# Pairs of the first MLP: three buffers for split weight forms, outputs written over copies, and conversion steps spread by time

## The chip, the core and the metric

The kernel runs on one core of a Trainium2 chip. The metric is the device time of one execution in microseconds (us). The profile is that of one further execution, taken by the hardware profiler.

## What is computed

An attention over a small state is followed by two MLPs. The 4608 rows (8 blocks of 512 sequence rows and 32 state rows) have 512 columns, and each MLP goes to 2048 columns and back.

```python
scores = scale * np.matmul(x, state.transpose(0, 1, 3, 2))
...
xread = np.matmul(a, state)
...
sread = np.matmul(a2, x)
x = np.concatenate([xread, sread], axis=2).transpose(0, 2, 1, 3).reshape(B * S, H * D)
h = x @ moe_w_in;  x = np.maximum(h, 0.0) ** 2 @ moe_w_out
h = x @ moe2_w_in; g = np.where(h > 0.0, h, np.exp(np.minimum(h, 0.0)) - 1.0)
return g @ moe2_w_out
```

All is float32 in its result, and the weights arrive as 64-bit numbers.

## The kernel before

**Precision.** A float32 operand is split into a rounded high part and a low remainder: ScalarE copies (L176), VectorE subtracts (L177). A product of two such operands is three matmuls (`product`, L41; L171 to L173).

**Stages.** Blocks 0 and 1 run alone. Blocks 2 to 7 run as three pairs of blocks (`pair`, L652), and this is the stage that the change touches. The 256 state rows follow, then the second MLP for all blocks.

**A pair.** 32 hidden steps (`h_step`, L657) make the hidden values: TensorE multiplies, ScalarE applies relu and square (L665, L666). Then the output product is made from seven products of 2 x 2 blocks instead of eight (`out_products`, L49): forms 1, 2, 6, 5, 7, 4, 3, each of eight steps. A step loads one weight (`weight1`, L645, tile `wr`, eight buffers), splits one operand into `gp` (four buffers) and runs six matmuls. Forms 6, 7 and 3 need a difference of hidden values first (`sub`, L82 and L83, on VectorE). Sums that are needed again are copied out of PSUM (L73, pools `eu` and `u2`) and later added into an output tile `o` (`added`, L76, L79; pool `oo1`, two buffers), which is stored (L678). The 16 last hidden steps run beside the first 16 product steps. The last 16 product steps of the first and second pair run beside the first eight hidden steps of the next pair, two to each.

**Conversion in the background.** The second MLP's weights are converted meanwhile, in 14 pairs of slices (`conv_pair`, L284). The raw slice (`raw`, two buffers) is read by L229 and L231 on ScalarE and becomes a float32 slice `cv` in four VectorE instructions; two more raw slices are asked for (`next_load`), the slices are stored as `d`, four sums are made (`sums`, L262), and `put_split` (L272) splits seven forms in four pieces. Each piece is copied by ScalarE into a tile `wf` (L279), subtracted by VectorE (L280) and stored (L281). In this stage `wf` has one buffer: `depth.update(raw=2, wf=1, cv=2)`. The code between two `yield` is run by one call of `next_conv` (L330). A pair takes seven calls.

**The order of the work.** Python lists `bg[i]` say what is called at step i: i below 16 is a hidden step, 16 to 31 a hidden step with a product step, 32 to 71 a product step alone. `CALLS = [27, 33, 40]` calls are spread evenly over the 72 steps of each pair (L699, L700). A scheduler then orders each engine's instructions by its own estimate of times. Every engine, and SyncE's queue of DMA issues (SP), runs its instructions in that order: one that waits holds up those behind it.

Of the kernel before, what the change touches and what calls it, by code (L numbers as in the profile page):

```python
# [34 lines left out]
HI, LO = 0, 1  # L35
SINGLE = 2
IN_SINGLE = 2
CALLS = [27, 33, 40]


def product(nc, ps, w, x, last, start):  # L41
# [7 lines left out]
def out_products(nc, split, g, weight, unit, put, sbuf, psum):  # L49


    gp_p, eu_p, u2_p, oo_p = sbuf
    tt, act = nc.vector.tensor_tensor, nc.scalar.activation
    count = iter(range(NF * HF))

    def phase(f, src, ps, start, combine=None):
        for j in range(HF):
            jj, r = divmod(j, 2)
            if combine and r == 0:
                combine(jj)  # L60
            if r % unit == 0:
                t = gp_p.tile([P, 2, unit, S], F32R, name="gp", tag="gp")
                split(t[:, HI], t[:, LO], src[jj][:, r:r + unit])
            w = weight(j, f)
            for m in range(2):
                sl = slice(m * P, (m + 1) * P)
                product(nc, ps[m], [(w[:, HI, sl], w[:, LO, sl])], [(t[:, HI, r % unit], t[:, LO, r % unit])],
                        j == HF - 1, start and j == 0)
            yield next(count)

    def copied(ps, p, name):
        t = p.tile([P, S], F32, name=name, tag=name)
        act(out=t, in_=ps, func=AF.Copy)  # L73
        return t

    def added(e, half, ps, u):  # L76
        for m in range(2):
            o = oo_p.tile([P, S], F32, name="o", tag="o")
            tt(out=o, in0=ps[m], in1=u[m], op=ALU.add)  # L79
            put(e, 2 * half + m, o)  # L80

    def sub(out, a, b):  # L82
        return lambda jj: tt(out=out[jj], in0=a[jj], in1=b[jj], op=ALU.subtract)  # L83

    a11, a12, a21, a22 = (g[q] for q in (11, 12, 21, 22))
    def banks(n):
        return [psum[n].tile([P, S], F32, name="xyz"[n], tag="xyz"[n]) for _ in range(2)]

    x = banks(0)
    yield from phase(1, a11, x, True)  # L90
    p1 = [copied(t, eu_p, "eu") for t in x]
    y = banks(1)
    yield from phase(2, a12, y, True)
    added(0, 0, y, p1)
    yield from phase(6, a11, x, False, sub(a11, a21, a11))
    u2 = [copied(t, u2_p, "u2") for t in x]
    z = banks(2)
    yield from phase(5, a21, z, True)
    yield from phase(7, a21, x, False, sub(a21, a22, a11))
    u3 = [copied(t, eu_p, "eu") for t in x]  # L100
    added(1, 1, z, u3)
    yield from phase(4, a22, x, False)
    for m in range(2):
        o = oo_p.tile([P, S], F32, name="o", tag="o")
        act(out=o, in_=x[m], func=AF.Copy)
        put(1, m, o)
    yield from phase(3, a12, z, False, sub(a12, a12, a11))
    added(0, 1, z, u2)


@with_exitstack
def attn_mlp_kernel(ctx: ExitStack, tc: tile.TileContext, xt, xn, st, w1, v1, w2, v2, outx, outs):
# [69 lines left out]
    if True:  # L182
# [88 lines left out]

        def put_split(w, srcs):  # L272

            first = 0
            for n, src in srcs:
                yield
                h = turn("wf", [P, n, 2, 256], F32R, "wf")
                with tc.issue_after(pace[0].ins):
                    nc.scalar.activation(out=h[:, :, HI], in_=src, func=AF.Copy)  # L279
                nc.vector.tensor_tensor(out=h[:, :, LO], in0=src, in1=h[:, :, HI].bitcast(F32), op=ALU.subtract)  # L280
                nc.sync.dma_start(out=w[:, first:first + n], in_=h.bitcast(F32))  # L281
                first += n

        def conv_pair(name, j):  # L284

# [1 line left out]
            v = [conv_p["cv"].tile([P, 512], F32, name="cv", tag="cv") for _ in range(2)]  # L287
            for _ in zip_longest(convert(name, j, v[0]), convert(name, j + HF, v[1])):
                yield
            next_load()  # L290
            next_load()
            d = wd[name, j] = dram.tile([P, 2, 512], F32, name=f"d_{name}{j}", tag=f"d_{name}{j}")
            for r in range(2):
                nc.sync.dma_start(out=d[:, r], in_=v[r])
            for t in sums(v):
                yield
            w = wf[name, j] = dram.tile([P, NF, 2, 256], F32, name=f"f_{name}{j}", tag=f"f_{name}{j}")
            yield from put_split(w, ((1, v[0][:, :256].unsqueeze(1)), (2, v[1].rearrange("p (q f) -> p q f", q=2)),
                                     (2, t[:, :2]), (2, t[:, 2:])))
# [266 lines left out]
        for b in range(SINGLE):  # L566
# [16 lines left out]
            else:  # L583
# [1 line left out]
                at(5, emit_m, b, 2)  # L585
                at(9, emit_m, b, 3)
                for i in range(18):
                    for _ in range(int('211212112112112110'[i])):
                        at(i, next_conv)
            at(13, emit_m, nb, 0)  # L590
            if nb < SINGLE:
# [42 lines left out]
        gq1_p = [pool(f"gq{q}", FC // 4) for q in range(4)]  # L634
        gap(pool, "gap4", 48)
        gp1_p = pool("gp1", 4)
        wr1_p = pool("wr1", 8)
        turns.update(raw=0, wf=0)
        depth.update(raw=2, wf=1, cv=2)
        conv_p.update(raw=pool("raw2", 1), cv=pool("cv2", 2), tf=pool("tf2", 1))  # L640
        eu1_p = pool("eu1", 2)
        u21_p = pool("u21", 2)
        oo1_p = pool("oo1", 2)
        ps_y, ps_x, ps_z = [pool(n, 2, space=bass.MemoryType.PSUM) for n in ("psy1", "psx1", "psz1")]
        def weight1(j, f):  # L645
            t = wr1_p.tile([P, 2, 256], F32R, name="wr", tag="wr")
# [5 lines left out]
        def pair(b0, bg, order):  # L652
# [25 lines left out]
                nc.sync.dma_start(out=x2d[b0 + e][:, k], in_=o)  # L678

            def products():  # L680
                for n in out_products(nc, split, g, weight1, 1, put, (gp1_p, eu1_p, u21_p, oo1_p), (ps_x, ps_y, ps_z)):
                    background(FC + n)
                    yield n

# [8 lines left out]
        for p, b in enumerate(pairs):  # L693
# [2 lines left out]
            def at(i, fn, *a):  # L696
                bg[i].append(lambda: fn(*a))

            for i in range(72):  # L699
                for _ in range((i + 1) * CALLS[p] // 72 - i * CALLS[p] // 72):  # L700
                    at(i, next_conv)
            for q in range(1, 4):
                at(4 * q - 3, emit_m, b, q)
                at(4 * q + 13, emit_m, b + 1, q)
# [387 lines left out]
```

## Time and profile before

| what | value |
|---|---|
| runs | 1345.14 us median of 3 (1344.6 to 1348.93) |
| the profiled execution | 1353.65 us, span 1351.9 us |
| TensorE (PE) | busy 1311.6 us, 97% |
| VectorE (DVE) | busy 968.0 us, 72% |
| ScalarE (ACT) | busy 877.4 us, 65% |
| DMA | 320.09 MB, mean 237 GB/s |

The span reaches from the first to the last instruction. Matmuls are pipelined and their ends are modelled, so a busy TensorE isn't always at its peak; its idle time and its granted clock tell more. Releasers of a wait are inferred from semaphores.

### The profile page before, as it was taken

The numbers are of one execution on the slowest core, as the hardware profiler recorded it, in microseconds if no ns is written. First come the engines' busy times: TensorE is split into PE (matmuls) and PEld (weight loads), VectorE is DVE, ScalarE is ACT, GpSimd is POOL, SyncE is SP. The second block draws the span as 40 slices with busy tenths as digits, with TensorE's granted clock in tenths as the row PEclk, the third lists the DMA queues.
The fourth block names the chain that finished last, engine by engine and source line by source line (L and its number), as shares of the span: only waits on it lengthen the run. The fifth ranks groups of instructions, "written<-read, shape, count | busy, mean of one in ns | idle before, by whom it ended". The sixth has DMA issues, their size and how long they took to land.

```text
span 1351.9 us, 19819 instructions
## 1 busy us (share of the span) xinstructions
PE 1311.6 (97%) x6972; PEld 1041.1 (77%) x6972; DVE 968.0 (72%) x1441; ACT 877.4 (65%) x1489; POOL 0.7 (0%) x6
## 2 busy tenths in 40 slices
PE   8999999999998999978999999999999999999999
PEld 6677766767666676767898888888888888888889
DVE  6988875897578975786656884569637894468645
ACT  5996768766775678754556843567446854576444
POOL 0000000000000000000000000000000000000000
PEclk9999999999999999989999999999999999999999
DMA  7999794588666886688977677876787777778733
GB/s 261 319 317 385 279 316 159 149 307 285 216 199 201 293 257 204 199 282 252 325 244 244 193 210 220 272 194 191 214 263 227 198 218 222 210 194 286 223 121 119
DMA packets 150002, 320.09 MB, mean 237 GB/s; under 512 B 15632, under 2 KB 36112, under 8 KB 146832
## 3 DMA queue, kind: packets, MB, share of 16 engines
q1 hardware_dynamic: 149904, 318.83, 74.3%
q8 instruction: 56, 0.92, 0.3%
q14 instruction: 42, 0.34, 0.1%
HBM read 242.22 MB, written 76.55 MB: 236 GB/s over the span
## 4 chain that ended last, share of the span: by engine, by line
PE 72%; DMA 9%; DVE 7%; ACT 5%; issue 1%; SPq 1%; ACTq 0%; DVEq 0%
PE x L45 20%; PE X L45 13%; PE z L45 9%; PE Z L45 6%; PE y L45 4%; PE Y L45 3%; PE h L171 3%; PE h L173 3%; PE h L172 2%; DMA f_w<-wf 2%; DMA raw_v<-in_v_dram 2%; PE as L45 2%; PE mp L350 1%; PE hs L45 1%; PE acc L171 1%
## 5 line engine op out<-in xcount | busy, mean ns | idle before, releaser
L45 PE MATMUL x<-gp,wr 128*128 128x512 f32 x1344 | 329.1, 398 | 15.2 <-DVE gp L177 9.6
L177 DVE TENSOR_TENSOR gp<-g,gp 128x512 fp32r<-128x512 f32 (+1 forms) x280 | 250.3, 901 | 124.3 <-ACT gp L176 123.0
L176 ACT ACTIVATE gp<-g 128x512 fp32r<-128x512 f32 (+1 forms) x280 | 221.3, 800 | 151.9 <-PE x L45 83.7
L45 PEld LDWEIGHTS x<-gp,wr 128*128 128x128 f32 x1344 | 254.2, 191 | 80.2 <-DVE gp L177 13.7
L45 PE MATMUL X<-xf,wr 128*128 128x512 f32 x768 | 186.6, 390 | 0.0
L45 PEld LDWEIGHTS X<-xf,wr 128*128 128x128 f32 x768 | 143.5, 188 | 31.5 <-ACT u L878 1.1
L45 PE MATMUL z<-gp,wr 128*128 128x512 f32 x672 | 157.6, 391 | 2.0 <-DMA wr<-p_v 1.5
L45 PEld LDWEIGHTS z<-gp,wr 128*128 128x128 f32 x672 | 126.2, 189 | 32.3 <-DVE gp L177 2.7
L874 DVE SCALAR_TENSOR_TENSOR g<-r,g 128x512 f32<-128x512 f32 x96 | 63.9, 689 | 65.1 <-ACT r L873 65.1
L171 PE MATMUL h<-at,m 128*128 128x512 f32 x256 | 103.4, 405 | 6.1 <-ACT m L176 3.9
L83 DVE TENSOR_TENSOR g<-g,g 128x1024 f32<-128x1024 f32 x84 | 102.1, 1219 | 0.6
L173 PE MATMUL h<-at,m 128*128 128x512 f32 x256 | 101.4, 397 | 0.0
L172 PE MATMUL h<-at,m 128*128 128x512 f32 x256 | 100.9, 394 | 0.0
L45 PE MATMUL Z<-xf,wr 128*128 128x512 f32 x384 | 97.4, 389 | 0.0
L872 ACT ACTIVATE r<-g 128x512 f32<-128x512 f32 x96 | 57.5, 625 | 58.7 <-DVE g L922 41.8
L45 PEld LDWEIGHTS Z<-xf,wr 128*128 128x128 f32 x384 | 72.1, 188 | 15.0
L873 ACT ACTIVATE r<-r 128x512 f32<-128x512 f32 x136 | 81.5, 620 | 0.7
L45 PE MATMUL y<-gp,wr 128*128 128x512 f32 x336 | 80.8, 389 | 0.0
L171 PEld LDWEIGHTS h<-at,m 128*128 128x128 f32 x256 | 48.6, 190 | 32.7 <-ACT m L176 5.2
L45 PEld LDWEIGHTS y<-gp,wr 128*128 128x128 f32 x336 | 63.1, 188 | 13.2
L665 ACT ACTIVATE g<-h 128x512 f32<-128x512 f32 x96 | 57.3, 600 | 18.5 <-PE h L173 17.8
L878 ACT ACTIVATE eu<-X 128x512 f32<-128x512 f32 x64 | 37.9, 593 | 42.8 <-PE X L45 42.8
(147 smaller groups left out, 1951.0 us busy)
## 6 DMA issues: line engine op xcount, KB each, us to landing
wr<-f_v SPq DMA_DIRECT2D x320, 256.0 KB, 3.2
wr<-f_w SPq DMA_DIRECT2D x224, 256.0 KB, 3.0
f_v<-wf SPq DMA_DIRECT2D x40, 512.0 KB, 4.3
wr<-p_v SPq DMA_DIRECT2D x72, 256.0 KB, 4.7
raw_w<-in_w_dram SPq DMA_DIRECT2D x32, 512.0 KB, 5.6
raw_v<-in_v_dram SPq DMA_DIRECT2D x32, 512.0 KB, 5.5
f_w<-wf SPq DMA_DIRECT2D x24, 512.0 KB, 3.7
xt<-in_xt_dram SPq DMA_DIRECT2D x8, 1024.0 KB, 6.9
```

The source lines that it names most:

```text
L45: nc.tensor.matmul(ps, wk[a], xk[b], start=start and k == 0 and i == 0, stop=last and k == len(w) - 1 and i == 2, skip_group_check=True)
L83: return lambda jj: tt(out=out[jj], in0=a[jj], in1=b[jj], op=ALU.subtract)
L171: mm(ps, w[HI], x[LO], start=first, stop=False)
L172: mm(ps, w[HI], x[HI], start=False, stop=False)
L173: mm(ps, w[LO], x[HI], start=False, stop=last)
L176: copy = nc.scalar.activation(out=hi, in_=src, func=AF.Copy)
L177: nc.vector.tensor_tensor(out=lo, in0=src, in1=hi.bitcast(F32), op=ALU.subtract)
L665: pace[:] = [nc.scalar.activation(out=h, in_=ps, func=AF.Relu)]
L872: act(out=r, in_=h, func=AF.Relu, scale=-1.0)
L873: act(out=r, in_=r, func=AF.Exp, scale=-1.0)
L874: nc.vector.scalar_tensor_tensor(out=out, in0=r, scalar=-1.0, in1=h, op0=ALU.add, op1=ALU.max)
L878: act(out=t, in_=ps, func=AF.Copy)
```

## The change

Four things are changed in the stage of the pairs, and some of it in the blocks before.

- `wf` gets three buffers (one and a pool of two), and `wr` seven instead of eight.
- The pool `oo1` is dropped. A sum is written over the copy that it was made from (`u[m]`), and the two plain outputs after form 4 use the pool `eu`.
- `put_split` asks for a piece's store one call later, so that a pair takes eight calls; `conv_pair` asks for the next loads and for the stores of `d` behind the sums, one call later.
- The numbers of calls are 32, 40 and 42. They are spread by a share for each step: 6 for a hidden step, 16 for a hidden step with a product, 10 for a product, 30 for the first eight steps of the second and third pair. The first two pairs stop at step 56, the third at 66. In block 1, 26 calls stand instead of 23.

```diff
@@ -35,7 +35,7 @@
 HI, LO = 0, 1
 SINGLE = 2
 IN_SINGLE = 2
-CALLS = [27, 33, 40]
+CALLS = [32, 40, 42]
 
 
 def product(nc, ps, w, x, last, start):
@@ -75,7 +75,7 @@
 
     def added(e, half, ps, u):
         for m in range(2):
-            o = oo_p.tile([P, S], F32, name="o", tag="o")
+            o = oo_p.tile([P, S], F32, name="o", tag="o") if oo_p else u[m]
             tt(out=o, in0=ps[m], in1=u[m], op=ALU.add)
             put(e, 2 * half + m, o)
 
@@ -101,7 +101,8 @@
     added(1, 1, z, u3)
     yield from phase(4, a22, x, False)
     for m in range(2):
-        o = oo_p.tile([P, S], F32, name="o", tag="o")
+        p, name = (oo_p, "o") if oo_p else (eu_p, "eu")
+        o = p.tile([P, S], F32, name=name, tag=name)
         act(out=o, in_=x[m], func=AF.Copy)
         put(1, m, o)
     yield from phase(3, a12, z, False, sub(a12, a12, a11))
@@ -271,29 +272,33 @@
 
         def put_split(w, srcs):
 
-            first = 0
+            first, store = 0, []
             for n, src in srcs:
                 yield
+                for args in store:
+                    nc.sync.dma_start(**args)
                 h = turn("wf", [P, n, 2, 256], F32R, "wf")
                 with tc.issue_after(pace[0].ins):
                     nc.scalar.activation(out=h[:, :, HI], in_=src, func=AF.Copy)
                 nc.vector.tensor_tensor(out=h[:, :, LO], in0=src, in1=h[:, :, HI].bitcast(F32), op=ALU.subtract)
-                nc.sync.dma_start(out=w[:, first:first + n], in_=h.bitcast(F32))
+                store = [dict(out=w[:, first:first + n], in_=h.bitcast(F32))]
                 first += n
+            yield
+            nc.sync.dma_start(**store[0])
 
         def conv_pair(name, j):
 
 
             v = [conv_p["cv"].tile([P, 512], F32, name="cv", tag="cv") for _ in range(2)]
             for _ in zip_longest(convert(name, j, v[0]), convert(name, j + HF, v[1])):
+                yield
+            for t in sums(v):
                 yield
             next_load()
             next_load()
             d = wd[name, j] = dram.tile([P, 2, 512], F32, name=f"d_{name}{j}", tag=f"d_{name}{j}")
             for r in range(2):
                 nc.sync.dma_start(out=d[:, r], in_=v[r])
-            for t in sums(v):
-                yield
             w = wf[name, j] = dram.tile([P, NF, 2, 256], F32, name=f"f_{name}{j}", tag=f"f_{name}{j}")
             yield from put_split(w, ((1, v[0][:, :256].unsqueeze(1)), (2, v[1].rearrange("p (q f) -> p q f", q=2)),
                                      (2, t[:, :2]), (2, t[:, 2:])))
@@ -585,7 +590,7 @@
                 at(5, emit_m, b, 2)
                 at(9, emit_m, b, 3)
                 for i in range(18):
-                    for _ in range(int('211212112112112110'[i])):
+                    for _ in range(int('221212112112112121'[i])):
                         at(i, next_conv)
             at(13, emit_m, nb, 0)
             if nb < SINGLE:
@@ -634,13 +639,13 @@
         gq1_p = [pool(f"gq{q}", FC // 4) for q in range(4)]
         gap(pool, "gap4", 48)
         gp1_p = pool("gp1", 4)
-        wr1_p = pool("wr1", 8)
+        wr1_p = pool("wr1", 7)
         turns.update(raw=0, wf=0)
-        depth.update(raw=2, wf=1, cv=2)
+        depth.update(raw=2, wf=3, cv=2)
         conv_p.update(raw=pool("raw2", 1), cv=pool("cv2", 2), tf=pool("tf2", 1))
         eu1_p = pool("eu1", 2)
         u21_p = pool("u21", 2)
-        oo1_p = pool("oo1", 2)
+        conv_p.update(wf=pool("wf2", 2))
         ps_y, ps_x, ps_z = [pool(n, 2, space=bass.MemoryType.PSUM) for n in ("psy1", "psx1", "psz1")]
         def weight1(j, f):
             t = wr1_p.tile([P, 2, 256], F32R, name="wr", tag="wr")
@@ -678,7 +683,7 @@
                 nc.sync.dma_start(out=x2d[b0 + e][:, k], in_=o)
 
             def products():
-                for n in out_products(nc, split, g, weight1, 1, put, (gp1_p, eu1_p, u21_p, oo1_p), (ps_x, ps_y, ps_z)):
+                for n in out_products(nc, split, g, weight1, 1, put, (gp1_p, eu1_p, u21_p, None), (ps_x, ps_y, ps_z)):
                     background(FC + n)
                     yield n
 
@@ -696,9 +701,15 @@
             def at(i, fn, *a):
                 bg[i].append(lambda: fn(*a))
 
-            for i in range(72):
-                for _ in range((i + 1) * CALLS[p] // 72 - i * CALLS[p] // 72):
+            share = [6] * FC + [16] * FC + [10] * (NF * HF - FC)
+            if p:
+                share[:HF] = [30] * HF
+            end = 66 if b + 2 == B else 56
+            done = 0
+            for i in range(end):
+                for _ in range(done * CALLS[p] // sum(share[:end]), (done + share[i]) * CALLS[p] // sum(share[:end])):
                     at(i, next_conv)
+                done += share[i]
             for q in range(1, 4):
                 at(4 * q - 3, emit_m, b, q)
                 at(4 * q + 13, emit_m, b + 1, q)

```

Lines below the changes move by 1 to 11: L176 is L177 in the change, L229 and L231 are L230 and L232, L279 is L282, L281 is L279 and L287, L214 is L215, L294 is L301, L649 is L654, L665 and L666 are L670 and L671, L678 is L683.

The first place is ScalarE's order in the first pair, where the last hidden steps end and products go on alone (`h1` is a hidden product in PSUM, `g1` hidden values, `gp` a product's operand, `cv` and `tf` the sources of the forms). Before:

```order
L665 ACTIVATE g1_2966<-h1_2985 128x512
L279 ACTIVATE wf_3006<-cv_2709 128x256
L666 ACTIVATE g1_2966<-g1_2966 128x512
L176 ACTIVATE gp_3096<-g1_2254 128x512
L229 ACTIVATE cv_3188<-raw_w24_2868 128x512
L176 ACTIVATE gp_3108<-g1_2284 128x512
L176 ACTIVATE gp_3124<-g1_2284 128x512
L279 ACTIVATE wf_3088<-cv_2710 128x2x256
L229 ACTIVATE cv_3189<-raw_w212_2870 128x512
L176 ACTIVATE gp_3140<-g1_2338 128x512
L176 ACTIVATE gp_3173<-g1_2338 128x512
```

And in the change:

```order
L670 ACTIVATE g1_2988<-h1_3011 128x512
L282 ACTIVATE wf_3138<-cv_2975 128x256
L671 ACTIVATE g1_2988<-g1_2988 128x512
L282 ACTIVATE wf_3170<-cv_2976 128x2x256
L177 ACTIVATE gp_3127<-g1_2254 128x512
L232 ACTIVATE raw_w25_3066<-raw_w25_3066 128x512
L232 ACTIVATE raw_w213_3068<-raw_w213_3068 128x512
L282 ACTIVATE wf_3219<-tf_3034 128x2x256
L230 ACTIVATE cv_3283<-raw_w25_3066 128x512
L177 ACTIVATE gp_3142<-g1_2284 128x512
L177 ACTIVATE gp_3158<-g1_2284 128x512
```

Two form copies have moved together, and two L232, a third form copy and an L230 stand in a row before the next operand copies.

The second place is SP's order near the end of the third pair (`p_v` and `f_v1` are the weights that products load, `f_v2` the stored forms, `d_v2` the stored slices, `eu` and `o` outputs). Before:

```order
L281 DMA f_v26_6234<-wf_6300 128x1024
L294 DMA d_v27_6396<-cv_6341 128x512
L649 DMA wr_6405<-f_v16_1601 128x512
L649 DMA wr_6419<-f_v17_1680 128x512
L649 DMA wr_6437<-p_v18_1079 128x2x256
L281 DMA f_v26_6234<-wf_6336 128x1024
L649 DMA wr_6457<-p_v19_1163 128x2x256
L649 DMA wr_6469<-p_v110_1231 128x2x256
L678 DMA x2d7_145<-o_6427 128x512
L678 DMA x2d7_145<-o_6430 128x512
L281 DMA f_v27_6415<-wf_6445 128x512
L649 DMA wr_6484<-p_v111_1315 128x2x256
```

And in the change:

```order
L683 DMA x2d7_145<-eu_6318 128x512
L683 DMA x2d7_145<-eu_6320 128x512
L279 DMA f_v27_6291<-wf_6375 128x1024
L654 DMA wr_6407<-f_v16_1658 128x512
L654 DMA wr_6418<-f_v17_1707 128x512
L287 DMA f_v27_6291<-wf_6401 128x1024
L654 DMA wr_6437<-p_v18_1079 128x2x256
L654 DMA wr_6453<-p_v19_1163 128x2x256
L654 DMA wr_6465<-p_v110_1234 128x2x256
L654 DMA wr_6476<-p_v111_1315 128x2x256
L654 DMA wr_6488<-p_v112_1419 128x2x256
L683 DMA x2d7_145<-eu_6427 128x512
```

Before, the pieces of the last two converted pairs (`f_v26`, `f_v27`) stand among the last eight weight loads (`p_v18` to `p_v115`). In the change the last piece, `f_v27`, stands ahead of them.

## Rows read from the trace of the kernel before

**Rows 1.** Windows: busy us by engine (instructions), TensorE's clock, DMA share, GB/s.
```profile
206.00:650.00 444.00, 415.89 (x2342) 309.23 (x2341) 331.31 (x556) 309.92 (x567) 0.00 (x0) 0.97 0.71 233
575.00:600.00 25.00, 19.80 (x74) 15.17 (x73) 20.64 (x36) 12.04 (x21) 0.00 (x0) 0.86 0.84 269
625.00:650.00 25.00, 21.44 (x110) 18.28 (x110) 12.19 (x25) 9.52 (x20) 0.00 (x0) 0.93 0.78 259
690.00:1290.00 600.00, 599.97 (x2654) 494.85 (x2653) 409.00 (x461) 352.51 (x521) 0.00 (x0) 1.00 0.77 226
```

**Rows 2.** Timeline: start, us, engine, line; in brackets idle before and releaser.
```profile
352.12 0.63 ACT L279 ACTIVATE wf<-tf 128x512 fp32r<-128x512 f32 x1 [0.85 <-DMA f_w<-wf]
354.13 0.50 PE L171 MATMUL h<-at,m 128*128 128x512 f32 x1 [1.97 <-DVE o L79]
...
430.75 0.63 ACT L279 ACTIVATE wf<-tf 128x512 fp32r<-128x512 f32 x1 [8.03 <-DMA f_w<-wf]
...
433.38 2.63 PE L45 MATMUL x<-gp,wr 128*128 128x512 f32 x6 [4.37 <-DVE gp L177]
```

**Rows 3.** Timeline of ScalarE and TensorE before three other gaps.
```profile
471.19 0.65 ACT L231 ACTIVATE raw_v<-raw_v 128x512 int32<-128x512 uint32 x1 [1.41 <-DMA raw_v<-in_v_dram]
472.38 1.88 PE L45 MATMUL x<-gp,wr 128*128 128x512 f32 x7 [1.34 <-ACT eu L73]
...
510.17 0.63 ACT L279 ACTIVATE wf<-tf 128x512 fp32r<-128x512 f32 x1 [3.81 <-DMA f_v<-wf]
513.56 0.69 ACT L231 ACTIVATE raw_v<-raw_v 128x512 int32<-128x512 uint32 x1 [1.12 <-DMA raw_v<-in_v_dram]
515.30 0.50 PE L171 MATMUL h<-at,m 128*128 128x512 f32 x1 [3.16 <-ACT m L176]
...
580.76 0.42 ACT L279 ACTIVATE wf<-cv 128x256 fp32r<-128x256 f32 x1 [6.08 <-DMA f_v<-wf]
583.33 0.65 ACT L231 ACTIVATE raw_v<-raw_v 128x512 int32<-128x512 uint32 x1 [2.15 <-DMA raw_v<-in_v_dram]
585.27 5.49 PE L45 MATMUL x<-gp,wr 128*128 128x512 f32 x12 [3.64 <-DVE gp L177]
```

**Rows 4.** Chain of waits, 575 to 590 us: start, us, what.
```profile
576.68 6.63 DMA raw_v<-in_v_dram
```

**Rows 5.** Waits of TensorE, 200 to 665 us: total us, times, longest.
```profile
PE x L45 <- DMA wr<-f_v: 4.2, 2, 2.1
PE z L45 <- DMA wr<-p_v: 1.5, 1, 1.5
```

**Rows 6.** Waits of ScalarE, 200 to 655 us.
```profile
ACT wf L279 <- DMA f_v<-wf: 22.0, 12, 6.1
ACT wf L279 <- DMA f_w<-wf: 15.2, 7, 8.0
ACT raw_v L231 <- DMA raw_v<-in_v_dram: 9.0, 6, 2.1
ACT raw_w L231 <- DMA raw_w<-in_w_dram: 5.4, 5, 2.3
```

**Rows 7.** Waits of SyncE's queue, 200 to 655 us.
```profile
SPq L281 <- DVE wf L280: 103.9, 43, 6.6
SPq L214 <- DVE cv L236: 18.3, 18, 2.2
```

**Rows 8.** DMA issues, 206 to 650 us: count, KB each, us to landing.
```profile
raw_v<-in_v_dram SPq DMA_DIRECT2D x16, 512.0 KB, 5.5
```

**Rows 9.** DMA, 550 to 575 us, then 287 to 340: totals, weight loads.
```profile
DMA packets 1966, 3.96 MB, mean 158 GB/s; under 512 B 210, under 2 KB 393, under 8 KB 1963
wr<-f_v SPq DMA_DIRECT2D x10, 256.0 KB, 3.3
...
DMA packets 7434, 15.59 MB, mean 294 GB/s; under 512 B 718, under 2 KB 2651, under 8 KB 7172
wr<-f_v SPq DMA_DIRECT2D x18, 256.0 KB, 5.0
```

## The prediction

> **What bounds the kernel now.** I read the windows first, by stage. In the stage of the pairs (206 to 650 us) TensorE is busy 415.89 of 444 us, so it stands idle for 28.1 us, and its mean granted clock of 0.97 costs up to 0.03 x 444 = 13.3 us more; in the stage after it (690 to 1290) it is idle for 0.03 us of 600 at clock 1.00 [rows 1]. So about 41 us can be had in the stage that the change touches, and none behind it. The clock part lies in single stretches of 25 us: five read 0.93, which is 1.75 us each (350, 425, 500, 600 and 625; the last stands for them), and 575 to 600 reads 0.86, 3.5 us [rows 1]. Before each of them TensorE had stood still.
>
> Next I read the timeline before each gap. The reader should look for who stood first. At 430.75 ScalarE stands 8.03 us before a form copy (L279) until the store of the form before it has landed, because there is one form buffer; the next operand copies (L176) stand behind it, and TensorE is idle for 4.37 us. At 354.13 TensorE is idle for 1.97 us behind an output sum on VectorE (L79), and just before it, at 352.12, a form copy had come 0.85 us late for the same reason, and its subtraction stood ahead of that sum [rows 2]. At 515.30 and 585.27 TensorE is idle for 3.16 and 3.64 us. There ScalarE stood at a form copy too (3.81 and 6.08 us), but what ended last was the wait of L231 for its weight load (1.12 and 2.15 us); at 472.38 such a load alone, 1.41 us of ScalarE, cost 1.34 us of TensorE [rows 3]. The chain shows that the load in front of 585.27 was asked for at 576.68, right behind the conversion that frees its buffer, and took 6.63 us [rows 4]. Three times it waits for product weights, 4.2 us at two places and 1.5 at the third [rows 5]. In all, ScalarE waits 22.0 + 15.2 = 37.2 us for form stores and 9.0 + 5.4 = 14.4 us for loads [rows 6]. SyncE's queue stands 103.9 us, 43 times, at a form store (L281) whose subtraction isn't done, and 18.3 us at loads whose buffer isn't read yet (L214); weight loads stand behind both [rows 7].
>
> **The change part by part.** A step of one product is six matmuls, and 2654 of them take 600 us [rows 1]: 6 x 0.226 = 1.36 us. A converted pair needs eight calls instead of seven, and 114 calls stand where 100 did; the instructions and transfers of a pair stay the same, so no engine gets more work, only other places for it.
>
> (a) Three form buffers instead of one. A form's buffer is free a step and a landing after its copy, and is wanted three forms on, so the two gaps of 4.37 and 1.97 us lose their cause: 6.3 us. Of the two clock stretches behind them (1.75 us each) a part is the gap itself; I take half, 1.75. Gain 8.1, bounds 0 and 9.8.
>
> (b) The load waits. The three gaps are 3.16 + 3.64 + 1.34 = 8.1 us, the clock behind them 1.75 + 3.5 = 5.25, together 13.4. The form copy ahead of L231 no longer stands, and the load is no longer asked for while its buffer is being read. But load and reader move together, and a load lands 5.5 us after its request [rows 8]. The bounds are 0 (L231 simply stands where the form copy stood) and 13.4. The nearest row is the wait at 471.19, a load with nothing before it, worth 1.34 us: each gap falls to that, 8.1 - 4.0 = 4.1, with half of the clock, 2.6. Gain 6.7.
>
> (c) Stores and loads a step later, and no conversions in the last six steps of the last pair. SyncE then meets stores whose data are ready, and the weights behind them are asked for sooner; in the new order the last form store stands ahead of the last eight weight loads. The three gaps are 5.7 us, their two clock stretches 3.5, together 9.2. I take 80%, 7.4, because a buffer less (seven weights) asks for them one step, 1.36 us, later. Bounds 0 and 9.2.
>
> (d) What comes new. The scheduler knows no wait at the forms any more and lays them closer. Where the interleaved steps end, ScalarE's order now has two form copies (0.42 us for a half and 0.63 for a whole one [rows 2, 3]), an operand copy, and then both L231, a third form copy and an L229, taken as long as an L231, before the next operand copies: 0.69 + 0.67 + 0.63 + 0.69 = 2.7 us in a row [rows 2, 3], some 3.7 with the two ahead. Four operand buffers give a lead of at most 4 x 1.36 = 5.4 us, and a load wait of up to 2.3 us [rows 6] does not fit into the remaining 1.7. I charge each of the three pairs one gap as at 472.38: 3 x 1.34 = 4.0. Bounds 0 (the lead covers it) and 3 x (1.34 + 1.75) = 9.3 with the clock behind each.
>
> (e) At nothing: outputs written over the copies. Sums and copies are as many as before. The tightest reuse is the copies after form 4, eight products (10.9 us) behind the sums stored from the same buffers; a landing as long as a load's, 5.5 us [rows 8], fits twice. The weight copies d are stored a step later, and their buffers are wanted only by the next pair, some five calls on. If that cover is gone, ScalarE stands at the copy (L73).
>
> Sum: 8.1 + 6.7 + 7.4 - 4.0 = 18.2 us, of the profiled execution's 1353.65 us (span 1351.9). The median of the runs is 1345.14, 8.5 us less. If those 8.5 us are stalls that only the profiled execution had, 33 of 41 us are there, a factor of 0.79; if not, 1. I take 0.9: 18.2 x 0.9 = 16.4, so **1329 us**. A measurement of this kernel tells changes over about 0.3% (4 us) from none, so faster means under 1341.1 and slower over 1349.2.
>
> One rule of the Trainium skill reads the stage otherwise. "Perfetto Trace Analysis", section "Identifying the Most-Contended Engine", takes busy matmuls for a bad measure of the headroom and LDWEIGHTS busy time for a good one. Loads are busy 309.23 of 444 us here and 494.85 of 600 in the later stage; at the later share of 82.5% the stage would need 375 us and lose 69 rather than 41. The rows do not bear that out as a gain: this stage also holds attention's small matmuls with short loads, which the change leaves alone. By the rule a sum that takes the same share of 69 would be 28 us, inside the first rival.
>
> **The rivals.** *All of it goes* (0.18). Loads are asked for early enough that L231 never stands, and the lead covers (d): 9.8 + 13.4 + 9.2 = 32.4, x 0.9 = 29 us, 1316 us. For it speaks that each gap at a load had a form copy standing before it or a late request; against it 472.38, which had no form copy before it.
>
> *The load takes the place of the store* (0.13). ScalarE comes to L231 sooner and stands there instead; more conversion per us in the pure products makes loads land later. Then (b) is nothing, (a) and (c) are halved to 4.0 and 4.6, and (d) costs 6: 2.6 us, x 0.9, 1343 us, no change. Weight loads did land later where more was moved: 5.0 us at 294 GB/s, 3.3 at 158 [rows 9]. "DMA: Bandwidth & Descriptors", section "Latency and other measured facts", in the Trainium skill has access to memory lengthen under high load; the trace agrees in direction. That three buffers do not work as three is no case of its own: they rotate over two pools of one and two, and that would end here too.
>
> *Slower* (0.09). SyncE's queue still stands at form stores, since a store asked for a step later can still come ahead of its subtraction, and weights now have seven buffers. The lead of a weight is 7 x 1.36 = 9.5 us; a landing of 5.0 leaves 4.5 for standing. It decides where SyncE stands longer than that; the mean is 103.9 / 43 = 2.4 now. If it happens once in each of the 14 pairs, each costs the lost step: 14 x 1.36 = 19 us, with (c) nothing, (d) 4.0, and (a) and (b) as forecast: 19 + 4.0 - 14.8 = 8.2, 1353 us. Against it: in the new order the stores lie whole products behind their copies.
>
> **How the numbers follow.** The forecast has 0.60, its own range 1321 to 1336 (sums of 10 to 24 us). Forecast and first rival are faster, 0.78; the second is the same, 0.13; the third slower, 0.09. The range reaches from 1315, just below the first rival, to 1345, past the second, and leaves out the third and the first rival's far side.
>
> **What would show it.** Right: waits of L279 for form stores under 8 us in the stage (37.2 now); SyncE's waits at form stores under 40; TensorE's idle time near 16 us of the stage and its clock at 0.98 or more; the span near 1335. (b) is wrong if L231's waits grow past 20 us; (c) if gaps before products still end on weight loads; (d) if no gap stands where the interleaved steps end. The whole is wrong if ScalarE's waits fall as said and TensorE's idle time does not.

## The result, and the profile after

The changed kernel takes 1331.0 us, median of 5 runs (1328.15 to 1337.93), against 1345.14 (1342.03 to 1348.93) for the kernel before: a ratio of 0.9898, 95% interval 0.9863 to 0.9933. A second comparison, on another chip (e8 below), gave 0.9886, 0.9865 to 0.9906. The forecast of 1329 us, a ratio of 0.988, lies inside both; its direction, range and likeliest case held. What the waits did in detail is less tidy, and the experiments are about that.

The profiled execution took 1328.15 us, with a span of 1326.4. That is 25.5 us less than the profiled execution of before, where the medians differ by 14.1: that execution lay 8.5 us above its median and this one 2.9 below its own. Single traces here differ by more than some of the parts that follow, so sizes are taken from medians, and causes from traces.

In after.py the lines of before have moved: L279 (form copy) is L282, L280 (its subtraction) L283, L281 (form store) L279 and, for the last form, L287; L231 (the conversion's second copy) is L232, L214 (raw load) L215, L176 and L177 (operand copy and subtraction) L177 and L178, L649 (product weights) L654.

The windows of after, in the columns of [rows 1] (the last row is before's, for 650 to 690 us):

```profile
206.00:650.00 444.00, 430.50 (x2541) 327.79 (x2540) 350.23 (x601) 323.63 (x609) 0.00 (x0) 1.00 0.76 254
425.00:450.00 25.00, 22.18 (x163) 15.25 (x164) 22.55 (x42) 15.04 (x28) 0.00 (x0) 1.00 0.92 319
575.00:600.00 25.00, 23.17 (x103) 19.16 (x103) 23.77 (x39) 17.36 (x32) 0.00 (x0) 1.00 0.93 313
650.00:690.00 40.00, 40.00 (x255) 35.94 (x254) 22.94 (x42) 22.61 (x48) 0.00 (x0) 1.00 0.75 265
690.00:1290.00 600.00, 599.89 (x2685) 496.01 (x2684) 408.28 (x456) 350.43 (x513) 0.00 (x0) 1.00 0.73 215
...
650.00:690.00 40.00, 37.55 (x315) 37.05 (x315) 31.25 (x64) 24.51 (x61) 0.00 (x0) 0.96 0.73 253
```

TensorE's idle time in the stage is 13.5 us (28.1 before), its clock there 1.00 (0.97 before), and the stage behind it is as full as it was. Fixed windows don't hold the same work in two kernels. The same work lies between the first product of the stage and the first product of the second MLP, here in the timeline of before and of after:

```profile
221.61 1.07 PE L45 MATMUL x<-gp,wr 128*128 128x512 f32 x4
695.54 0.84 PE L45 MATMUL X<-xf,wr 128*128 128x512 f32 x3
```

```profile
225.08 1.30 PE L45 MATMUL x<-gp,wr 128*128 128x512 f32 x5
670.06 0.84 PE L45 MATMUL X<-xf,wr 128*128 128x512 f32 x3
```

It took 473.9 us and takes 445.0, 28.9 less, while the stage before it gave 3.5 back. In e8, the same kernel traced again, it takes 449.5, 24.5 less. Some of this lies where the sum did not look: in 650 to 690 us TensorE was busy 37.55 of 40 at clock 0.96 in the profiled execution of before, and is busy all the time now.

The waits of after, 206 to 650 us (engine, line and what it waited for: us in total, times, longest), first ScalarE's, to lay beside [rows 6], then SyncE's, beside [rows 7], then TensorE's, beside [rows 5]:

```profile
ACT raw_v L232 <- DMA raw_v<-in_v_dram: 18.6, 10, 4.4
ACT raw_w L232 <- DMA raw_w<-in_w_dram: 3.9, 5, 1.9
ACT wf L282 <- DMA f_w<-wf: 2.3, 2, 1.2
ACT wf L282 <- DMA f_v<-wf: 2.2, 2, 1.5
...
SPq L279 <- DVE wf L283: 71.4, 31, 8.8
SPq L215 <- DVE cv L237: 24.6, 20, 4.3
SPq L287 <- DVE wf L283: 6.5, 6, 1.5
...
PE x L45 <- DVE gp L178: 6.7, 6, 1.8
PE sc L355 <- DMA xt<-in_xt_dram: 2.4, 1, 2.4
PE z L45 <- DMA wr<-f_v: 1.1, 1, 1.1
```

Four readings. ScalarE's waits for form stores fell from 37.2 to 4.5 us. Its waits for raw loads **grew**, from 14.4 to 22.5. SyncE still stands 71.4 us at form stores and 6.5 at the last one of each converted pair (L287), 77.9 in all. And TensorE waits 1.1 us for weights where it waited 5.7.

The costliest place left is the end of the last pair's interleaved steps. The timeline of after there, 564 to 577 us (rows of other instructions left out):

```profile
568.77 0.94 SPq L215 DMA_DIRECT2D raw_v<-in_v_dram  x2
569.23 0.42 DVE L267 TENSOR_TENSOR tf<-cv 128x256 f32<-128x256 f32 x1
569.90 1.29 DVE L178 TENSOR_TENSOR gp<-g,gp 128x512 fp32r<-128x512 f32 x2
570.64 4.40 PE L45 MATMUL x<-gp,wr 128*128 128x512 f32 x18 [1.61 <-DVE gp L178]
574.40 0.65 ACT L232 ACTIVATE raw_v<-raw_v 128x512 int32<-128x512 uint32 x1 [4.42 <-DMA raw_v<-in_v_dram]
575.48 1.65 ACT L177 ACTIVATE gp<-g 128x512 fp32r<-128x512 f32 x3
576.87 1.42 PE L45 MATMUL x<-gp,wr 128*128 128x512 f32 x5 [1.83 <-DVE gp L178]
```

Read from below: TensorE is idle for 1.83 us at 576.87, because the operand copies of 575.48 stood behind an L232 that had waited 4.42 us for a load asked for at 568.77. Six us earlier it was idle for 1.61 us, because VectorE had taken a conversion and its sums (L267 and others) before the operand's subtraction. The end of the first pair's interleaved steps shows the same on a smaller scale, in the timeline of 272 to 286 us:

```profile
272.96 1.61 SPq L215 DMA_DIRECT2D raw_w<-in_w_dram  x2
278.14 0.72 ACT L232 ACTIVATE raw_w<-raw_w 128x512 int32<-128x512 uint32 x1 [1.86 <-DMA raw_w<-in_w_dram]
281.89 1.13 ACT L177 ACTIVATE gp<-g 128x512 fp32r<-128x512 f32 x2
283.38 2.81 PE L45 MATMUL x<-gp,wr 128*128 128x512 f32 x11 [1.31 <-DVE gp L178]
```

Here ScalarE has the order that stood on record as the first place: form copies, both L232, a form copy and an L230 ahead of the operand copies of 281.89. TensorE is idle for 1.31 us behind them. The second pair has no such gap. The other large gap is in the timeline at 434 us, where the next batch's scores wait for their input, a load of 1 MB asked for at 426.87:

```profile
426.87 0.38 SPq L197 DMA_DIRECT2D xt<-in_xt_dram  x1
434.46 1.01 PE L355 MATMUL sc<-xt,st 64*32 64x512 f32 x2 [2.43 <-DMA xt<-in_xt_dram]
```

### The profile page after: what moved, and what is told of

Read it like the earlier page. It is cut to its first block, busy times and chain, and to the rows that moved or that the text cites. A ratio compares the mean times of both kernels' runs of the same rounds, so it can differ in the third digit from the quotient of the medians.

```text
span 1326.4 us, 19848 instructions
## 1 busy us (share of the span) xinstructions
PE 1300.5 (98%) x6972; PEld 1034.9 (78%) x6972; DVE 964.6 (73%) x1441; ACT 873.4 (66%) x1489; POOL 0.7 (0%) x6
## 4 chain that ended last, share of the span: by engine, by line
PE 80%; DMA 7%; DVE 6%; ACT 6%; issue 2%; SPq 1%; POOLq 0%; ACTq 0%; DVEq 0%; POOL 0%
PE x L45 20%; PE X L45 13%; PE z L45 11%; PE Z L45 7%; PE y L45 4%; PE h L172 3%; PE h L174 3%; PE h L173 3%; PE Y L45 3%; PE mp L355 2%; PE as L45 2%; DMA raw_v<-in_v_dram 2%; PE hs L45 1%; DMA raw_w<-in_w_dram 1%; PE acc L172 1%
## 5 line engine op out<-in xcount | busy, mean ns | idle before, releaser
L178 DVE TENSOR_TENSOR gp<-g,gp 128x512 fp32r<-128x512 f32 (+1 forms) x280 | 250.1, 901 | 121.6 <-ACT gp L177 120.6
L45 PE MATMUL x<-gp,wr 128*128 128x512 f32 x1344 | 322.3, 392 | 6.8 <-DVE gp L178 6.7
L177 ACT ACTIVATE gp<-g 128x512 fp32r<-128x512 f32 (+1 forms) x280 | 220.9, 799 | 158.1 <-PE x L45 84.0
L45 PEld LDWEIGHTS x<-gp,wr 128*128 128x128 f32 x1344 | 250.1, 188 | 70.5 <-DVE gp L178 9.4
L670 ACT ACTIVATE g<-h 128x512 f32<-128x512 f32 x96 | 56.9, 594 | 17.4 <-PE h L174 16.9
```

What stands on the lines that cost most here:

```text
L45: nc.tensor.matmul(ps, wk[a], xk[b], start=start and k == 0 and i == 0, stop=last and k == len(w) - 1 and i == 2, skip_group_check=True)
L177: copy = nc.scalar.activation(out=hi, in_=src, func=AF.Copy)
L178: nc.vector.tensor_tensor(out=lo, in0=src, in1=hi.bitcast(F32), op=ALU.subtract)
L670: pace[:] = [nc.scalar.activation(out=h, in_=ps, func=AF.Relu)]
```

## The experiments

Each ran beside the kernel before on its chip; a ratio is to that, with its 95% interval.

| kernel | median us (runs) | ratio | interval |
|---|---|---|---|
| changed kernel | 1331.0 (5) | 0.9898 | 0.9863 to 0.9933 |
| e8, the same again | 1332.42 (4) | 0.9886 | 0.9865 to 0.9906 |
| e1, three buffers alone | 1341.56 (6) | 0.9956 | 0.9940 to 0.9973 |
| e2, times alone | 1345.43 (12) | 0.9979 | 0.9962 to 0.9997 |
| e3, store at once | 1336.49 (6) | 0.9923 | 0.9903 to 0.9944 |
| e4, even spread | 1331.73 (5) | 0.9878 | 0.9856 to 0.9900 |
| e6, third raw buffer | 1334.35 (4) | 0.9899 | 0.9873 to 0.9924 |
| e7, loads sooner | 1336.13 (6) | 0.9911 | 0.9889 to 0.9933 |
| e9, stores on GpSimd | 1345.49 (11) | 0.9983 | 0.9969 to 0.9996 |
| e10, L232 at its step | 1329.89 (6) | 0.9874 | 0.9846 to 0.9901 |
| e11, paced by operands | 1322.28 (5) | 0.9809 | 0.9785 to 0.9833 |
| e12, and scores later | 1318.67 (5) | 0.9780 | 0.9757 to 0.9804 |
| e13, one form buffer | 1341.84 (12) | 0.9964 | 0.9942 to 0.9986 |

### One part alone: e1 and e2

The kernel before with the buffers only:

```diff
-wr1_p = pool("wr1", 8)
+wr1_p = pool("wr1", 7)
...
-depth.update(raw=2, wf=1, cv=2)
+depth.update(raw=2, wf=3, cv=2)
...
-oo1_p = pool("oo1", 2)
+conv_p.update(wf=pool("wf2", 2))
```

with the outputs written over the copies, as in the change.

> The kernel before with three form buffers, seven weight buffers and outputs over the copies; stores, loads and conversion steps stay where they were. Theory of the prediction (the buffers carry term (a) and half of term (b), the later stores and the times of the steps carry term (c)): ScalarE's waits at form copies fall from 37.2 us to under 8 in the stage, SyncE's at form stores stay near 100, the gaps before products on weight loads stay (5.7 us), so 8.1 + 3.4 = 11.5, less one lost step or two for the eighth weight buffer: about 10 us, 1335 us. Rival one, the buffers are the whole of it: 1331, and TensorE's idle time in 206 to 650 us falls to about 14. Rival two, the places are the whole of it: 1345 within 4, with ScalarE standing at the conversion's copy (L231 of before) for 25 us or more instead.

Measured: 0.9956, 5.9 us less, between the theory's 10 and nothing. The waits of e1 in the stage:

```profile
ACT raw_v L232 <- DMA raw_v<-in_v_dram: 16.9, 8, 3.8
ACT raw_w L232 <- DMA raw_w<-in_w_dram: 6.4, 5, 1.8
...
SPq L282 <- DVE wf L281: 64.7, 35, 9.1
...
PE x L45 <- DMA wr<-f_v: 3.8, 2, 3.2
PE z L45 <- DMA wr<-p_v: 1.5, 2, 1.1
PE z L45 <- DMA wr<-f_v: 0.6, 1, 0.6
```

No row of a form copy waiting for a store is left (for its source it waits 6.0 us): 37.2 us of waiting are gone, for 5.9 us of time. L232 stands 23.3 us where it stood 14.4, so part of rival two came true as a wait, though not as a time. The gaps on weights stay, 5.9 us (5.7 before), as said. SyncE's standing fell to 64.7 though no store had moved; the theory had it at 100.

The kernel before with the changed kernel's shares and ends of the conversion steps, and nothing else:

```diff
-for i in range(72):
-    for _ in range((i + 1) * CALLS[p] // 72 - i * CALLS[p] // 72):
+share = [6] * FC + [16] * FC + [10] * (NF * HF - FC)
...
+end = 66 if b + 2 == B else 56
```

> The kernel before, only the conversion steps placed by time (the shares and the ends at steps 56 and 66), with its old number of calls; one form buffer, stores at once, loads early. Theory: ScalarE still stands 30 us or more at form copies for the one buffer, the gaps like those of 4.37 and 3.64 us stay, only the last six steps without conversions give something: 1341 to 1345. Rival, the places carry the gain: 1333, TensorE's idle time in the stage under 18 us and ScalarE's waits at forms under 15.

Measured: 0.9979, 2.0 us less in the medians: the places carry little by themselves, as the theory had it. ScalarE still waits 36.1 us at form copies.

### One part taken out: e3, e4, e7, e13

e3 asks for each form store in the step of its copy; a pair then takes seven calls again, so the old numbers of calls, in block 1 too, go with it:

```diff
-    for args in store:
-        nc.sync.dma_start(**args)
...
-    store = [dict(out=w[:, first:first + n], in_=h.bitcast(F32))]
+    nc.sync.dma_start(out=w[:, first:first + n], in_=h.bitcast(F32))
```

> The changed kernel with each form store asked for in the step of its copy again (seven calls a pair, the old numbers of calls, the old string of the stage of single batches); three buffers, shares and later loads stay. Theory (term (c)): SyncE's waits at form stores go from 78 us to 100 or more, weights behind them come late again, 3 to 6 us of gaps on weight loads with clock behind: 1335 to 1338. Rival, SyncE's standing costs nothing since seven weight buffers cover it: within 3 us of the changed kernel, 1328 to 1334, although SyncE's waits grow as said.

Measured: 1336.49, a ratio of 0.9923 against 0.9886 and 0.9898: some 3 to 5 us of the gain hang on the later store. The intervals overlap; against e4 on the same chip, which is as fast as the changed kernel, it is 4.8 us. The size is the theory's, the reason isn't. In e3 SyncE waits at form stores and TensorE at weights like this:

```profile
SPq L282 <- DVE wf L281: 65.0, 31, 10.2
...
PE z L45 <- DMA wr<-f_v: 1.8, 2, 1.3
PE tp L421 <- DVE m L178: 4.2, 2, 2.1
```

SyncE stands no longer than in the changed kernel (65.0 and 77.9 us), and weights cost 2.0 us at TensorE, not 3 to 6. The one group that grew by more than a us is attention's transposes, held behind the split of its small operands (4.2 us; 1.1 in the changed kernel). One trace doesn't show that this is the cause; by which wait a store asked for at once costs time stays open.

e4 spreads the steps evenly again:

```diff
...
-for _ in range(done * CALLS[p] // sum(share[:end]), (done + share[i]) * CALLS[p] // sum(share[:end])):
...
+for _ in range((i + 1) * CALLS[p] // 72 - i * CALLS[p] // 72):
```

> The changed kernel with the conversion steps spread evenly over the 72 steps as before (32, 40 and 42 of them). Theory: three buffers and later stores keep the gains in the middle of the stage; conversions in the last six steps of the last pair come back and hold weights and the state rows' operands: 3 to 6 us, 1334 to 1337, lost behind 600 us of the span. Rival one, the shares matter everywhere (pure products have no room for evenly spread steps): 1340 or more with idle time spread over all pairs. Rival two, placing is worth nothing: 1331 within 3.

Measured: 0.9878, no slower than the changed kernel, though conversions stand in the last six steps again. Rival two holds: with three buffers and later stores the shares and ends are worth nothing that these runs can tell.

e7 asks for the loads ahead of the sums (the stores of `d` stay behind them, though its expectation counts them in):

```diff
-for t in sums(v):
-    yield
 next_load()
 next_load()
...
+for t in sums(v):
+    yield
```

> The changed kernel with the two next loads (and the weight copies) asked for ahead of the sums again, as in the kernel before. Theory (half of term (b) is the later request): SyncE stands longer at loads whose buffer is not read yet (31.1 us at L215 now, 40 or more then), weights behind them come later; 2 to 4 us slower, 1333 to 1336. Rival one, asked sooner they land sooner: ScalarE's waits at L232 fall from 22.5 to under 15 us and the time falls by 3 us or more. Rival two, the place of the request is worth nothing: within 2 us.

Measured: 1336.13 beside the changed kernel's 1332.42 on the same chip, 3.7 us, with overlapping intervals: likely the theory's size, not settled. Its profiled run, at 1330.83, is the fastest of its six, so the trace doesn't show the loss. L232 waits 28.3 us, and 27.1 in e8: asking sooner does not make it wait less, so rival one is out.

e13 leaves the changed kernel one form buffer:

```diff
-depth.update(raw=2, wf=3, cv=2)
+depth.update(raw=2, wf=1, cv=2)
...
-conv_p.update(wf=pool("wf2", 2))
+pool("wf2", 2)
```

> The changed kernel with one form buffer in place of three; stores and loads a step later, shares, seven weight buffers and outputs over the copies stay. Theory (terms (a) and (b) hang on the buffers): ScalarE stands at form copies again for 40 us or more, since a store asked for in the next step leaves its landing to be waited for; at least 14.8 x 0.9 = 13 us slower than the changed kernel, 1344 or more. Rival (later stores and loads alone carry the change): 1336 or less.

Measured: 1341.84, a ratio of 0.9964: some 9 to 10 us of the changed kernel's 14 to 15 go without the buffers. The direction is the theory's, the size two to four us below its bound. ScalarE's waits in e13:

```profile
ACT raw_v L232 <- DMA raw_v<-in_v_dram: 18.8, 10, 5.5
ACT wf L282 <- DMA f_v<-wf: 14.6, 14, 2.3
ACT raw_w L232 <- DMA raw_w<-in_w_dram: 11.5, 6, 4.0
ACT wf L282 <- DMA f_w<-wf: 9.7, 10, 2.9
```

At forms it waits 24.3 us, not over 40, and at most 2.9 at a time (8.0 in before); its waits for loads are 30.3.

### Where the rest is: e8, e6, e9

> The changed kernel itself once more, so that the next ones have it beside them on the same chip: 1331 within 4 us, ScalarE's waits at weight loads (L232) in 206 to 650 us near 20, at form copies under 6.

Measured: 1332.42, L232 27.1 us, form copies 5.3. The changed kernel's own rows repeat: gaps of 1.59 and 2.82 us at the end of the last pair's interleaved steps, 1.85 at the end of the first pair's, 2.9 at the scores.

e6 gives a form buffer to the raw weights:

```diff
-depth.update(raw=2, wf=3, cv=2)
-conv_p.update(raw=pool("raw2", 1), cv=pool("cv2", 2), tf=pool("tf2", 1))
+depth.update(raw=3, wf=2, cv=2)
+conv_p.update(raw=pool("raw2", 2), cv=pool("cv2", 2), tf=pool("tf2", 1))
...
-conv_p.update(wf=pool("wf2", 2))
+conv_p.update(wf=pool("wf2", 1))
...
-for _ in range(2):
+for _ in range(3):
     next_load()
```

> The changed kernel with three buffers for raw weights and two for forms (in place of two and three), and three loads asked for ahead, so that every other load comes a pair earlier. Theory (the waits at L232 that grew to 22.5 us are mostly covered by the four operand buffers): these waits fall to about 11 us, two form buffers already keep ScalarE's waits at form copies under 10, and the time stays within 4 us of the changed kernel's, 1327 to 1334. Rival one, the load wait took the place of the store wait and is what the stage still loses: half of the waits gone gives 5 us or more, 1326 or less. Rival two, the third form buffer is needed: form waits come back over 15 us and the time is 1336 or more.

Measured: 1334.35, ratio 0.9899. The expectation on the waits was wrong: L232 still stands 26.1 us, as long as in e8. The scheduler had moved the copy up with its load (in the trace all but one stand 5 to 8 us behind their load's request), so the experiment did not take the wait away and says nothing on its price. What it shows: with two form buffers ScalarE waits 10.9 us at form copies, and the time is within 2 us of the changed kernel's beside it.

e9 lets GpSimd ask for the form stores:

```diff
 for args in store:
-    nc.sync.dma_start(**args)
+    nc.gpsimd.dma_start(**args)
...
-nc.sync.dma_start(**store[0])
+nc.gpsimd.dma_start(**store[0])
```

> The changed kernel with the form stores asked for by GpSimd, which has nothing else to do there, so that SyncE's queue no longer stands at them (78 us in the stage now). Theory (term (c): the standing is what held weights back, and what is left of it is still paid): the gaps before products on weights (1.1 us) and the late large loads go, 2 to 4 us less, 1327 to 1329. Rival one, seven weight buffers cover the standing that is left: within 2 us of the changed kernel. Rival two, GpSimd's own asking of a 512 KB store takes longer and the stores land later, so that ScalarE stands at form copies again: slower by 3 us or more.

Measured: 1345.49, ratio 0.9983; rival two by size, though mostly by another place. SyncE no longer stands at form stores, and in the stage ScalarE waits 17.4 us for them (5.3 in e8), as that rival said. But the first product of the pairs comes at 231.1 us (223.2 in e8): some 8 of the 11.3 us between the two traces are lost before the pairs, where most form stores (`f_v`) now land 7.6 us after their request (4.5 in e8). So these runs don't show what SyncE's standing alone costs; they show that this way out costs more.

### The lump: e10, e11, e12

e10 binds the conversion's second copy to its step:

```diff
-with tc.issue_after(gate[0].ins) if gate else nullcontext():
+with tc.issue_after(after[0].ins) if after else nullcontext():
     nc.scalar.activation(out=low, in_=low.bitcast(U32), func=AF.Copy, scale=2.0 ** -29)
```

> The changed kernel with one line changed: the conversion's second copy (L232) may not come before the relu that its step follows, as already holds for L230. In the changed kernel that copy stands about 15 product matmuls (3.4 us) behind the request of its load, and a load lands 5.6 us after its request; with the edit all but six of them stand 37 matmuls (8 us) or more behind it. Theory (the load took the place of the store at ScalarE, and costs little, since gaps behind it are only the 1.8 us at 577): ScalarE's waits at L232 fall from 22.5 us to under 8, the time is 1 to 3 us less than the changed kernel's 1331 to 1332. Rival one, these waits are what the stage still loses (half of its 13.5 us idle): 6 us or more less, 1326 or under. Rival two, they are free, and something else is late: within 1 us or slower.

Measured: 1329.89, ratio 0.9874: 1 to 3 us less, which the runs don't tell from none. L232's waits fall from 22.5 to 9.9 us, not under 8, so most of this waiting was free. What stayed stands where the interleaved steps of the three pairs end: 2.9, 1.8 and 5.2 us. The first and the last in the timeline of e10:

```profile
272.72 0.69 ACT L232 ACTIVATE raw_w<-raw_w 128x512 int32<-128x512 uint32 x1 [2.31 <-DMA raw_w<-in_w_dram]
278.33 1.88 PE L45 MATMUL x<-gp,wr 128*128 128x512 f32 x7 [2.14 <-DVE gp L178]
...
569.07 0.94 SPq L215 DMA_DIRECT2D raw_v<-in_v_dram  x2
575.49 0.65 ACT L232 ACTIVATE raw_v<-raw_v 128x512 int32<-128x512 uint32 x1 [5.22 <-DMA raw_v<-in_v_dram]
577.96 1.43 PE L45 MATMUL x<-gp,wr 128*128 128x512 f32 x5 [2.62 <-DVE gp L178]
```

These two cost TensorE time: its gaps there are 2.14 us in the first pair, and 1.14 and 2.62 in the last. Behind the last relu the bound means nothing: the pure products have no relu, so there the scheduler may bunch the conversions. e11 lets the operand copies set the pace there too:

```diff
+def paced(*a):
+    pace[:] = [split(*a)]
...
-out_products(nc, split, g, weight1,
+out_products(nc, paced, g, weight1,
```

> As the one before, and the steps' conversions also may not come before the newest operand copy, so that in the pure products, where there is no relu, they can't bunch. Every L232 then stands 21 matmuls or more behind its load's request. Theory: the lump where the interleaved steps end (1.6 + 1.8 us of TensorE at 570 and 577 in the changed kernel) goes, ScalarE's waits at L232 fall under 4 us: 3 to 4 us less, 1327 to 1329. Rival, conversions that follow the operand copy of each step hold the next one: the gaps on operands (x products waiting on DVE, 6.7 us) grow past 10 us and the time is 1334 or more.

Measured: 1322.28, ratio 0.9809: 7.6 us less than e10 on the same chip, twice what the theory said, which had counted the last pair's gaps alone. The waits of e11 in the stage:

```profile
ACT raw_v L232 <- DMA raw_v<-in_v_dram: 1.2, 1, 1.2
...
PE x L45 <- DVE gp L178: 2.3, 3, 1.3
PE z L45 <- DMA wr<-f_v: 2.2, 1, 2.2
```

No form copy waits for a store, no gap stands at the end of the first or the last pair's interleaved steps (5.9 us in e10), products wait 2.3 us for operands (6.8 in e10), and from 455 us to the end of the stage TensorE's waits come to 0.5 us in all. The rest of the 7.6 us isn't traced to a place; the clock of the stage reads 0.99 in e10 and 1.00 in e11. The bunching was the largest thing left.

e12 is e11 with the second batch's scores later:

```diff
-for c, t in ((b + 2, 17), (b + 3, 38)):
+for c, t in ((b + 2, 17), (b + 3, 40)):
```

> As the one before, with the second batch's scores (and all that hangs on them) two steps later, so that its input, loaded four steps ahead, has 2.7 us more to land. Theory: the gap of 2.4 to 3.1 us at 431 us (scores waiting for the input) goes, in each of two pairs at most: 2 to 4 us less than the one before, about 1325. Rival: what hangs on the scores (the operand of the next pair, its first small matmuls) comes too late there: no gain.

Measured: 1318.67, ratio 0.9780, 3.6 us less than e11, as said; its five runs (1315.76 to 1318.83) all lie below the fastest run of the changed kernel, 1328.15. The stage's window of e12:

```profile
206.00:650.00 444.00, 437.24 (x2610) 333.75 (x2609) 360.39 (x616) 333.48 (x623) 0.00 (x0) 1.00 0.78 256
```

6.8 us of idle time are left of the 28.1 of before. This version beats both kernels.

## Why the prediction was right, and where it was not

**What bounds the kernel.** Right: all of the gain lies in the stage of the pairs and in the 40 us behind it, and the stage of the second MLP kept its length. The Trainium skill ("Perfetto Trace Analysis", section "Identifying the Most-Contended Engine") has the headroom read from LDWEIGHTS busy time. Held against the later stage's 82.5%, as in the prediction, that leaves the changed kernel's stage, with 327.79 us of 444, 47 us still to lose, and e12, with 333.75, 40. The traces don't bear that out: TensorE is idle for only 13.5 and 6.8 us there, at clock 1.00.

**(a)** and **(b)**, together 14.8 x 0.9 = 13.3 us on the buffers and the load requests. The mechanism is shown by e1 and e13, the size isn't: the buffers are worth 5.9 us put in alone and 9 to 10 taken out last. The step that failed is in (b), "the load is no longer asked for while its buffer is being read", from which L231 was to wait less. It waits more, 22.5 us, past the 20 that the text set as its own mark. The second rival's wait did come: load and reader move together, and by the order that e10's expectation gives, the reader stands some 15 matmuls (3.4 us) behind a request that takes 5.6 us to land. What saved the time is that these waits are mostly covered (e10). Why they are covered is not shown: the gaps of 3.16 and 3.64 us stood behind two waits in a row, form copy and load [rows 3], which speaks for the four operand buffers hiding one, but at 472.38 a single wait had cost 1.34 us.

**(c)**, 7.4 x 0.9 = 6.7 us for later stores and loads and no conversions in the last steps. The weight gaps fell from 5.7 us to 1.1, as said; the changed kernel with eight weight buffers was not run. By e3 and e7 the later stores are worth some 3 to 5 us and the later loads perhaps 3.7; by e4 the empty last steps are worth nothing that shows. The step that failed is "SyncE then meets stores whose data are ready": 77.9 us of standing, not under 40. SyncE's total standing was a poor measure: it is 77.9 us in the changed kernel and 65.0 in e3, which is slower.

**(d)**, 4.0 us for the new lump. The place was right, and the size nearly: two pairs of three show it, with 1.31 + 1.61 + 1.83 = 4.8 us, and 5.9 in e10. Taking the bunching away, in all the pure products, gave 7.6 us (e10 to e11), more than the term and within its bound of 9.3.

**(e)** held: no operand copy or product waits on an output sum's buffer in the changed kernel's stage.

**The sum.** 18.2 x 0.9 = 16.4 us against 14.1 and 15.1 measured. By the medians (a) and (b) were too large and (c) about right; the parts don't add up, since what one is worth hangs on the others. That the total came so near is in part luck. The 18.2 us were read off the profiled execution of before, and between the two events above the traces gave 28.9 (24.5 in e8); of that the medians keep half to six tenths, where the text took 0.9. A sum that was too small and a factor that was too large offset each other. Its signs for TensorE held (13.5 us idle, near 16 said; clock 1.00, 0.98 or more said), and the span, 1326.4 us where it said 1335, shows that surplus of the traces. Two slips in the working change no case: sums of 10 to 24 us times 0.9 end at 1324, not 1321, and the second rival halves (c) from its bound of 9.2 instead of from 7.4, which makes 1344 of its 1343. *Slower* did not happen: SyncE does stand at form stores, but its condition was more than 4.5 us at a time in each of the 14 pairs, and in the trace of after three stands are longer than that, 8.8 us the longest; TensorE waits 1.1 us for weights.

## What to carry to other kernels

A wait's total is no price: 37 us of waiting at a buffer bought 6 to 10 us, 13 us of waiting at loads bought 1 to 3, and the few waits where work bunched, some 8 us of ScalarE's in e10, were part of a lump whose removal gave 7.6. Look for the wait behind which the busy engine's operand stands, and ask what lets the work bunch there; a pacing rule that follows one kind of instruction ends where that kind ends. Read each part's price by putting it in alone and by taking it out last: here, for the buffers, one gave 5.9 and the other 9 to 10.

## What was not expected of the hardware

- Some loads in the stage land a little later with the denser work: product weights 5.3 us after their request at 254 GB/s, 4.9 before at 233. "DMA: Bandwidth & Descriptors", section "Latency and other measured facts", in the Trainium skill has access lengthen under load. The traces agree for these and for `xt` (7.3 us, 6.7 before); `raw_w` (5.4, 5.6 before) and `xn` (5.8, 6.8 before) landed sooner. The DMA issues of after, 206 to 650 us (count, KB each, us to landing):

```profile
wr<-f_v SPq DMA_DIRECT2D x96, 256.0 KB, 5.3
raw_v<-in_v_dram SPq DMA_DIRECT2D x16, 512.0 KB, 5.6
xt<-in_xt_dram SPq DMA_DIRECT2D x4, 1024.0 KB, 7.3
```

- With stores asked for by GpSimd other transfers landed later too: between 100 and 232 us of e9 the reads of converted weights (cv<-d_v) took 8.4 us to land, 5.4 in e8, though not all did (raw_w 5.0, 5.8 in e8). One trace of each doesn't show why.
- A gap's length alone did not decide the granted clock. In after TensorE stood idle for 2.43 us at 434 us, and 425 to 450 us read 1.00; the same stretch reads 0.93 in e8, with a gap of 2.90 us there, and 0.86 in e10, with one of 2.68. In after 200 to 225 us read 0.93, with a gap of 1.75 us at 202.58. In before a gap of 1.97 us at 354 stood in a stretch of 0.93.
